# Row maxima taken bank by bank, four of each unit's pairs through a difference of keys: a four-layer attention kernel on one NeuronCore

## The chip, the cores and the metric

The kernel runs on one core of a Trainium2 chip. The time is device microseconds from the first to the last instruction of one execution. The engines named below are the tensor engine (PE, with its weight loads listed apart as PEld), VectorE (DVE), ScalarE (ACT), GpSimd (POOL) and SyncE (SP), which issues the DMAs. PSUM, where PE writes, has eight banks of 512 float32 values per partition.

## The reference

Four layers stand one behind the other on an input of 2048 tokens by 576 features: A, B, A, B. Each adds the output of an attention block over the layer-normed input. A has 32 heads of 18 features with keys and values of their own; in B all heads share one key and one value. There is no mask.

```python
def _A_ref(x, wqkv, wo):                      # D, H = 576, 32; Dh = 18
    qkv = (x @ wqkv).reshape(B, S, 3, H, Dh)  # q, k, v per head
    scores = einsum("bhqd,bhkd->bhqk", q, k) * Dh ** -0.5
    o = einsum("bhqk,bhkd->bhqd", softmax(scores), v)
    return o.reshape(B, S, D) @ wo
# _B_ref: the same with one k and one v for all heads
x = x + _A_ref(layernorm(x), ...); x = x + _B_ref(layernorm(x), ...)   # twice
```

So each layer computes 32 score matrices of 2048 by 2048, their row maxima, their exponentials, the row sums and the product with the values, in float32.

## The kernel before, in words

Each layer has three parts. First the layer norm, the transposes of x and the projections; q and k go to DRAM split into a coarse and a fine half, so that 18 features become 54 rows (coarse, fine, coarse for q; coarse, coarse, fine for k) and one product of 54 rows gives the score to float32 accuracy. Then the attention loop. Last the output projection of the layer, which runs into the norm of the next.

The attention loop goes over 16 pairs of heads; the first head's rows lie on partitions 0 to 63 and the second's on 64 to 127, so that the matmuls of the two heads use different halves of the tensor engine. A **unit** is one pair of heads and 512 queries; a layer has 64 units, and each takes four steps over the engines:

1. **Maxima.** For each head, four blocks of 128 queries by four blocks of 512 keys: 32 matmuls (L542), each of which fills one PSUM bank with scores, queries on the partitions. Two of them, side by side in a tile of two banks (`psm`, two such tiles rotate), are reduced by one VectorE instruction over 128 x 1024 values (L551) into two columns of `mx`.
2. **The maximum as rows.** VectorE takes the negative maximum of each four columns (L682), GpSimd splits it into halves, VectorE transposes it, and two sets of DMAs bring it through DRAM into two rows of the q operand, beside rows of ones in k. The contraction of the next step then gives score minus maximum.
3. **Exponentials.** 32 matmuls (L706), each 128 keys by 512 queries, into single banks (`pse`, three rotate), and 32 ScalarE exponentials (L710) into SBUF tiles `pt`.
4. **Values.** For each 512 queries, eight steps of four matmuls of 19 columns (18 features and a column of ones for the sum) on the four column groups of the tensor engine, summed into the bank `oacc` (L731). One ScalarE copy (L737) takes the sum out, and GpSimd and DMAs finish it.

PSUM thus holds four banks for maxima, three for exponentials and `oacc`. The tiles of the first and last part of a layer come from the same two rings.

The order on the tensor engine is written out by hand. `UNIT` is a list of phases; each names a run of **rows** (`m0` is the next maximum matmul of the first head, `e1` the next exponential matmul of the second) and a number of columns of step 4 that follow them. The list of before has twelve phases with 32 maxima, 32 exponentials and 4096 columns in all, that is one unit. The maxima run 14 steps (56 matmuls) ahead of the exponentials; these 56 are woven into the projections ahead of the loop, and at its end the 56 exponentials that are left run three to a phase with 384 columns. Small work (DMAs, sums, loads of the next weights) hangs in a table `todo` by step. Semaphores are put in by the framework, from what each instruction reads and writes; the engines work through their queues in order.

```python
UNIT = [("m0 m1 e0 e0 e1 m0 m1", 384), ("e0 m1 m0 e1 e0", 352), ...]   # twelve phases
        rows, cols = UNIT[phase % len(UNIT)]
        for kind, a in rows: exp_next(a) if kind == "e" else max_mm()
        if phase >= 2: pv_cols(cols)
```

## Time and profile before

| | |
|---|---|
| median of three runs | 5763.13 us (5759.74 to 5768.0) |
| the profiled execution: time, span | 5768.38 us, 5766.5 us |
| mean granted clock of the tensor engine | 0.996 |
| busy: PE, DVE, ACT, POOL | 99%, 89%, 79%, 30% of the span |
| L551, maxima on VectorE | 4096 instructions, 4736.5 us busy, 1219 ns each |
| L710, exponentials on ScalarE | 8192 instructions, 4288.9 us busy, 602 ns each |
| L542 and L706, score matmuls | 8192 each, 452 and 433 ns each |

Busy time is the time in which an engine has at least one instruction in flight; instructions of an engine that follow each other closely overlap in part, so busy time divided by their count can be less than the duration of one. The ends of matmuls are modelled, and float32 matmuls (step 4) appear as two instructions each. The chain is followed back from the last instruction, at each step to what released it.

### The profile page before, as it was taken

The numbers are of one execution on the slowest core, as the hardware profiler recorded it, in microseconds if no ns is written. First come the engines' busy times: TensorE is split into PE (matmuls) and PEld (weight loads), VectorE is DVE, ScalarE is ACT, GpSimd is POOL, SyncE is SP. The second block draws the span as 40 slices with busy tenths as digits, with TensorE's granted clock in tenths as the row PEclk, the third lists the DMA queues.
The fourth block names the chain that finished last, engine by engine and source line by source line (L and its number), as shares of the span: only waits on it lengthen the run. The fifth ranks groups of instructions, "written<-read, shape, count | busy, mean of one in ns | idle before, by whom it ended". The sixth has DMA issues, their size and how long they took to land.

```text
span 5766.5 us, 141306 instructions
## 1 busy us (share of the span) xinstructions
PE 5734.9 (99%) x57918; PEld 2923.1 (51%) x57918; DVE 5117.8 (89%) x5321; ACT 4581.1 (79%) x8872; POOL 1735.3 (30%) x2224
## 2 busy tenths in 40 slices
PE   9999999999999999999999999999999999999999
PEld 8644444444844444444685444444448444444446
DVE  4799999998699999999638999999977999999995
ACT  2588888888388888888625888888882888888885
POOL 3133232324233323233311423232332332323232
PEclk9999999999999999999999999999999999999999
DMA  6311111111420000001243111111114100010002
GB/s 201 106 46 32 35 32 36 32 33 23 126 66 24 22 23 20 23 20 24 59 169 91 40 35 33 34 33 34 31 33 129 52 23 23 23 23 20 23 14 77
DMA packets 250340, 276.96 MB, mean 48 GB/s; under 512 B 131732, under 2 KB 171924, under 8 KB 239972
## 3 DMA queue, kind: packets, MB, share of 16 engines
q1 hardware_dynamic: 249692, 267.92, 16.9%
q8 instruction: 455, 7.45, 0.6%
q14 instruction: 193, 1.58, 0.1%
HBM read 151.24 MB, written 112.56 MB: 46 GB/s over the span
## 4 chain that ended last, share of the span: by engine, by line
PE 96%; ACT 1%; DVE 1%; POOL 1%; DMA 1%; issue 0%; SPq 0%; POOLq 0%; ACTq 0%; DVEq 0%
PE oacc L731 36%; PE pse L706 24%; PE psm L542 23%; PE psn L224 6%; PE psq L394 6%; ACT pt L710 1%; DVE mx L551 1%; PE ps L216 0%; DMA raw<-in_B_wk_dram 0%; POOL big L170 0%; SPq L157 0%; PE oacc L217 0%; POOL os L745 0%; POOL os L767 0%; POOL os L144 0%
## 5 line engine op out<-in xcount | busy, mean ns | idle before, releaser
L551 DVE TENSOR_REDUCE mx<-psm 128x2 f32<-128x1024 f32 x4096 | 4736.5, 1219 | 173.5 <-PE psm L542 158.3
L710 ACT ACTIVATE pt<-pse 128x512 f32<-128x512 f32 x8192 | 4288.9, 602 | 538.3 <-PE pse L706 404.4
L542 PE MATMUL psm<-big 62*128 62x512 f32 x8192 | 2538.4, 452 | 6.9 <-DVE mx L551 6.8
L706 PE MATMUL pse<-big 64*128 64x512 f32 x8192 | 2494.8, 433 | 4.0 <-DMA big<-m_d 2.9
L731 PE MATMUL oacc<-pt,vbuf 128*19 128x320 f32 (+5 forms) x27664 | 1787.6, 361 | 5.2 <-ACT oc L737 5.2
L706 PEld LDWEIGHTS pse<-big 64*128 64x128 f32 x8192 | 1225.7, 185 | 861.4 <-ACT pt L710 675.7
L542 PEld LDWEIGHTS psm<-big 62*128 62x128 f32 x8192 | 1052.7, 184 | 815.2 <-DVE mx L551 645.0
L731 PEld LDWEIGHTS oacc<-pt,vbuf 128*19 128x19 f32 x27664 | 537.2, 98 | 784.1 <-issue 603.4
L144 POOL TENSOR_SCALAR hl<-neg 128x8 fp32r<-128x8 f32 x256 | 50.9, 199 | 2631.2 <-DVE neg L682 2631.2
L754 POOL TENSOR_TENSOR rl<-lt,mone 128x8 f32<-128x8 f32 x256 | 423.7, 1655 | 576.5 <-DMA lt<-os 576.5
L731 PE MATMUL oacc<-pt,vy 128*19 128x192 f32 (+2 forms) x9200 | 595.2, 361 | 0.0
L144 POOL TENSOR_SCALAR os<-oc 32x512 f32<-32x512 f32 x512 | 314.4, 614 | 138.2 <-ACT oc L737 96.2
L767 POOL TENSOR_TENSOR os<-os,rb 96x512 f32<-96x512 f32 x256 | 329.5, 1287 | 22.6 <-DMA rb<-r_d 21.8
L745 POOL TENSOR_TENSOR os<-os,oc 96x512 f32<-96x512 f32 x256 | 328.3, 1282 | 21.3
L731 PEld LDWEIGHTS oacc<-pt,vy 128*19 128x19 f32 x9200 | 195.7, 98 | 273.4 <-issue 213.4
L402 ACT ACTIVATE ev<-psq 128x512 fp32r<-128x512 f32 (+1 forms) x112 | 67.0, 598 | 324.7 <-PE psq L394 235.4
L224 PE MATMUL psn<-wsm,xx 128*128 128x288 f32 x2240 | 307.4, 296 | 0.0
L224 PEld LDWEIGHTS psn<-wsm,xx 128*128 128x128 f32 x2240 | 298.6, 188 | 10.4 <-issue 7.1
L408 DVE TENSOR_TENSOR ev<-psq,ev 128x512 fp32r<-128x512 f32 (+1 forms) x84 | 58.1, 691 | 215.6 <-ACT ev L402 202.5
L394 PE MATMUL psq<-yx,big 128*128 128x512 f32 (+2 forms) x826 | 197.5, 392 | 5.3 <-DVE ev L408 2.5
L394 PE MATMUL psq<-xx,big 128*128 128x512 f32 (+1 forms) x784 | 194.2, 397 | 0.0
L737 ACT ACTIVATE oc<-oacc 128x512 f32<-128x512 f32 x256 | 158.1, 618 | 30.4 <-PE oacc L731 30.4
(73 smaller groups left out, 1380.7 us busy)
## 6 DMA issues: line engine op xcount, KB each, us to landing
big<-qk_d SPq DMA_DIRECT2D x180, 432.0 KB
qk_d<-ev SPq DMA_DIRECT2D x96, 512.0 KB
qk_d<-ev SPq DMA_DIRECT2D x120, 256.0 KB
rb<-r_d SPq DMA_DIRECT2D x512, 36.0 KB
o_d<-os SPq DMA_DIRECT2D x512, 36.0 KB
m_d<-tr SPq DMA_DIRECT2D x1024, 2.0 KB
o<-o_d SPq DMA_DIRECT2D x64, 256.0 KB
big<-m_d SPq DMA_DIRECT2D x512, 4.0 KB
```

What stands on the lines that cost most here:

```text
L144: eng.tensor_scalar(dst, src, 1.0, 0.0, op0=OP.mult, op1=OP.add)
L224: nc.tensor.matmul(ps, lhs[:, xc, :], wsm[:, wc, h * 288:(h + 1) * 288], start=i == 0, stop=i == len(TERMS) - 1)
L394: nc.tensor.matmul(ps[:n].rearrange("p (u t) -> p u t", u=2)[:, us], w[:, wc, :n], xts[T][:, us, xc, :], start=(xc, wc) == TERMS[0], stop= ...
L542: nc.tensor.matmul(ps[:, slot], q[b:b + KM, c0:c0 + P], k[b:b + KM, kb * 512:(kb + 1) * 512], start=True, stop=True)
L551: nc.vector.reduce_max(mxs[p, u][:, r0:r1 + 1:r1 - r0], ps, axis=AX.X)
L706: nc.tensor.matmul(e, k[r:r + KE, kc * P:(kc + 1) * P], q[r:r + KE, u * 512:(u + 1) * 512], start=True, stop=True)
L710: nc.scalar.activation(pt, e, AF.Exp, scale=SCALE)
L731: nc.tensor.matmul(oacc[j:j + DH + 1, cs], v_of(kc)[:, 2 * p + a if is_a else 0, :], pts[p, u, i][:, cs], start=kc < 2 and c0 == 0, stop=k ...
L737: nc.scalar.activation(oc, oacc, AF.Copy)
L745: nc.gpsimd.tensor_tensor(t[:96], t[:96], oc[:96], op=OP.add)
L754: nc.gpsimd.tensor_tensor(rl, lts.pop((p, u)), mone, op=OP.pow)
L767: nc.gpsimd.tensor_tensor(t[:96], t[:96], rb[:96], op=OP.mult)
```

## The change

The score matmuls and everything else that used the two PSUM rings now use one tile of seven banks, `banks`, and helper functions hand out its banks by number: in the loop banks 0 to 3 for exponentials and 4 to 6 for maxima, in the tail of a layer all seven for exponentials, elsewhere 0 to 2 for single tiles and 3 to 6 for pairs.

In the loop each maximum matmul has a bank and a reader of its own. Of the 32 of a unit, 24 are reduced by VectorE one bank at a time. The other eight are four pairs a, b with the same queries and two blocks of keys. The row maximum of both is the maximum of a + relu(b - a); the matmul for b takes the difference of the two blocks of keys as its operand, ScalarE writes its relu to SBUF, and VectorE adds that to the matmul of a and takes the maximum in one instruction (which the build turns into two: the sum with its maximum, and a read of the accumulator). The first pair of heads of each layer has no differences and reduces all 32 bank by bank.

The differences of keys are made once per pair of heads (in B once per layer): DMAs bring the halves of the two blocks into `xx`, GpSimd subtracts and splits them, and DMAs take them through DRAM into rows of `xx`. The weight loads inside the loop now share one of the two `xh` buffers; the other holds the relu. `UNIT` has ten phases with the same 32 maxima, 32 exponentials and 4096 columns. The tail runs four exponentials and 512 columns per phase, and its last copies of `oacc` move to VectorE.

```diff
-UNIT = [("m0 m1 e0 e0 e1 m0 m1", 384), ("e0 m1 m0 e1 e0", 352), ...
+UNIT = [("m1 e0 e1 e0 m1 m0", 512), ("m0 e1 m1 e0 e1 m0", 480), ("e1 m0 m1 e0 e0 m0 e1", 416),
+        ("m1 m0 e1 e0 e1 m0", 224), ("e1 m0 m1 m1 e0", 544), ("m1 m0 e0 e1 e1 m0", 352), ("e0 m1 e1 m0 e0 m1", 416),
+        ("m0 e1 e1 m1 e0 m1 e0", 384), ("m1 m0 e1 e0 m0 e0 e1 m1 m0", 448), ("m0 e1 m1 e0 m1 e0", 320)]
+UNIT_X = (9, 16, 24, 31)
...
+    banks = psum.tile([P, 7, 512], F32, name="banks")
...
-    def mtile2(name):
-        return psum.tile([P, 2, 512], F32, tag="m", bufs=2, name=name)
-    def etile(name):
-        return psum.tile([P, 512], F32, tag="e", bufs=3, name=name)
+    at_bank = {"e": 0, "m": 0, "pair": 0}
+    layout = {"e": 3, "m": 4}
+    def mtile2():
+        at_bank["pair"] += 1
+        i = 3 + 2 * (at_bank["pair"] % 2)
+        return banks[:, i:i + 2]
+    def m1tile():
+        at_bank["m"] += 1
+        return banks[:, 4 + at_bank["m"] % 3]
+    def etile():
+        at_bank["e"] = (at_bank["e"] + 1) % layout["e"]
+        return banks[:, at_bank["e"]]
...
+            if diff:
+                nc.tensor.matmul(ps, q[b:b + 3 * DH, c0:c0 + P], kd(p)[b:b + 3 * DH], start=True, stop=True)
+            else:
+                nc.tensor.matmul(ps, q[b:b + KM, c0:c0 + P], k[b:b + KM, kb * 512:(kb + 1) * 512], start=True, stop=True)
...
+                if diff:
+                    t = relus[p, u, a, qc] = relu[:, :512]
+                    nc.scalar.activation(t, ps, AF.Relu)
+                elif (p, u, a, qc) in relus and kb == 0:
+                    t = relus.pop((p, u, a, qc))
+                    nc.vector.tensor_tensor_reduce(t, ps, t, 1.0, LOWEST, OP.add, OP.max, mx[:, r:r + 1])
+                else:
+                    nc.vector.reduce_max(mx[:, r:r + 1], ps, axis=AX.X)
...
+        def diff_split(p):
+            nc.gpsimd.tensor_tensor(d, hi1, hi0, op=OP.subtract)
+            nc.gpsimd.tensor_tensor(d, d, lo1, op=OP.add)
+            nc.gpsimd.tensor_tensor(d, d, lo0, op=OP.subtract)
+            copy(nc.gpsimd, hi, d)
+            nc.gpsimd.tensor_tensor(lo, d, hi.bitcast(F32), op=OP.subtract)
...
-                    max_mm()
+                    max_mm(True)
...
+        layout.update(e=7)
         while sum(e_next) < 4 * ns:
             run_todo(LEAD + sum(e_next) // 4)
-            for _ in range(min(3, 4 * ns - sum(e_next))):
+            for _ in range(min(4, 4 * ns - sum(e_next))):
                 exp_next(int(e_next[0] > e_next[1]))
-            pv_cols(384)
+            pv_cols(512)
```

## The prediction

> **What bounds the kernel now.** I read the page first, then the groups of one long stretch of the loop, the chain there, and single rows.

> ```profile
> span 5766.5 us, 141306 instructions
> ...
> PE 5734.9 (99%) x57918; PEld 2923.1 (51%) x57918; DVE 5117.8 (89%) x5321; ACT 4581.1 (79%) x8872; POOL 1735.3 (30%) x2224
> ...
> PE 96%; ACT 1%; DVE 1%; POOL 1%; DMA 1%; issue 0%; SPq 0%; POOLq 0%; ACTq 0%; DVEq 0%
> ...
> L551 DVE TENSOR_REDUCE mx<-psm 128x2 f32<-128x1024 f32 x4096 | 4736.5, 1219 | 173.5 <-PE psm L542 158.3
> L710 ACT ACTIVATE pt<-pse 128x512 f32<-128x512 f32 x8192 | 4288.9, 602 | 538.3 <-PE pse L706 404.4
> L542 PE MATMUL psm<-big 62*128 62x512 f32 x8192 | 2538.4, 452 | 6.9 <-DVE mx L551 6.8
> ```

> The last line says that a maximum matmul hardly ever waits for its bank: 6.9 us in all. The groups from 600 to 1368 us:

> ```profile
> L551 DVE TENSOR_REDUCE mx<-psm 128x2 f32<-128x1024 f32 x636 | 735.3, 1219 | 26.4 <-PE psm L542 24.3 <-PE pse L706 1.0
> ...
> L737 ACT ACTIVATE oc<-oacc 128x512 f32<-128x512 f32 x40 | 24.7, 617 | 0.6 <-PE oacc L731 0.6
> ```

> 40 copies of `oacc`, one a unit, in 768 us: a unit takes 19.2 us. VectorE is busy 18.4 of them (735.3/40). The chain in this stretch lies on the tensor engine alone; its pieces (start, length) show two phases:

> ```profile
> 803.23 0.23 PE psm L542
> 803.46 0.24 PE pse L706 x2
> 803.70 0.82 PE oacc L731 x8
> ...
> 808.01 0.43 PE pse L706 x2
> 808.44 0.24 PE psm L542 x2
> 808.68 0.22 PE pse L706
> 808.90 0.56 PE oacc L731 x8
> ```

> Rows of the two heads run side by side; the first pair of a phase costs 0.43 us, each further one 0.235. Then 416 columns of step 4 take 0.82 and 256 take 0.56, so c columns take 0.14 + 1.63c/1000. The twelve phases need 35 such pairs: 12 x 0.43 + 23 x 0.235 + 12 x 0.14 + 4096 x 0.00163 = 18.9 us of the 19.2. The tensor engine's order is the bound and stalls 0.3 us a unit; VectorE is close behind.

> **The change: the rows.** From the new list of phases alone one would expect a gain (a rival, below). But before a row can be priced, one must know what it waits for. Waits come from the framework, and the built program lists them:

> ```
> L811 Matmult banks<-big 128x512 [waits DVE_49]
> L598 Matmult banks<-big 128x512 [waits Activation_49]
> L811 Matmult banks<-big 128x512 [waits DVE_49]
> L598 Matmult banks<-big 128x512 [waits Activation_49]
> L836 Matmult oacc<-pt,vbuf 19x416 x4
> L598 Matmult banks<-big 128x512 [waits DVE_49]
> L811 Matmult banks<-big 128x512 [waits DVE_49]
> L811 Matmult banks<-big 128x512 [waits Activation_49]
> ```

> L811 is an exponential row (banks 0 to 3, which only ScalarE reads there), L598 a maximum row. An exponential row behind a maximum row waits for VectorE, which reads none of its banks; a maximum row behind an exponential row waits for ScalarE. By the values of the semaphores it is the reader of the row directly ahead, in all but some 170 of the 16384 rows. So the seven banks are guarded as one tile: a row may start only when the row before it has been read. In the program of before each ring slot is a tile of its own, and `pse` waits for ScalarE alone. One place there has the same form, the two halves of a `psq` pair in the first layer, of which the second waits for the subtraction that reads the first:

> ```profile
> 20.98 0.69 DVE L408 TENSOR_TENSOR ev<-psq,ev 128x512 fp32r<-128x512 f32 x1 [1.75 <-ACT ev L402]
> ...
> 21.73 0.19 PEld L394 LDWEIGHTS psq<-yx,big 128*128 128x128 f32 x1
> ```

> That load starts 0.06 after the subtraction's end (21.67), and its record carries a wait for VectorE's semaphore, where the loads around it carry none. So such a wait for a neighbouring bank does reach the chip, though here it cost almost nothing.

> The price of a row is now a round trip, and rows of before that waited show its parts:

> ```profile
> 799.52 0.60 ACT L710 ACTIVATE pt<-pse 128x512 f32<-128x512 f32 x1
> ...
> 800.18 0.18 PEld L706 LDWEIGHTS pse<-big 64*128 64x128 f32 x1 [0.25 <-ACT pt L710]
> ...
> 769.54 0.51 PE L706 MATMUL pse<-big 64*128 64x512 f32 x2
> ...
> 770.08 2.58 ACT L710 ACTIVATE pt<-pse 128x512 f32<-128x512 f32 x5 [0.18 <-PE pse L706]
> ```

> From the end of a reader to the next weight load 0.06; from there to the start of the next reader 0.54. With the 0.60 of ScalarE an exponential row costs 1.20 us, and a relu row the same. For VectorE over 512 values I take the 0.69 of the subtraction above (between 0.61, half of 1.219, and 0.69 nothing changes that matters): 1.29. The sum with its maximum is not in the trace. Below, the plain 0.69 bounds it; above, 0.69 and a second full pass; I take 0.69 plus the 0.18 of the smallest reduction, since its second instruction reads one value:

> ```profile
> L682 DVE TENSOR_REDUCE neg<-mx 128x8 f32<-128x32 f32 x40 | 7.0, 176 | 0.0
> ```

> That makes 1.47 (1.29 to 1.98, over 960 of them +0.5 or -0.2 ms). The loops hold 4 x (2048 - 56) = 7968 exponentials and as many maxima, of which 960 are relus, 960 sums and 6048 plain. Sum: 8928 x 1.20 + 6048 x 1.29 + 960 x 1.47 = 19.93 ms, where the same 249 units (7968/32) took 249 x 19.2 = 4.78 ms. Behind a waiting row PE holds the rest of the phase and its columns of step 4; ScalarE and VectorE, which wait for just those rows, idle meanwhile. Step 4 waits for nothing new and runs while the last row of a phase is read; only the widest phases stick out (512 columns: 0.33 + 0.97 = 1.30 against 1.29), 0.05 ms. At the full clock the loops thus gain 15.2 ms in length.

> **The clock.** A round trip leaves the tensor engine idle most of the time: 64 matmuls of 0.5 and ten phases of step 4 of about 0.75 are some 39 us of an 80 us unit, 49% busy. These rows (a stretch, PE busy, ..., granted clock) show what followed such stretches:

> ```profile
> 1323.30:1326.76 3.46, 1.72 (x24) 0.68 (x22) 1.73 (x3) 1.83 (x4) 3.04 (x7) 1.00 0.05 15
> 1326.76:1330.17 3.41, 3.41 (x25) 1.35 (x21) 2.08 (x3) 1.73 (x4) 1.22 (x2) 0.50 0.10 21
> 1436.00:1439.40 3.40, 2.11 (x26) 0.72 (x28) 0.00 (x0) 2.58 (x6) 0.94 (x2) 1.00 0.25 76
> 1439.40:1442.80 3.40, 3.40 (x27) 0.87 (x19) 2.86 (x2) 2.70 (x6) 2.97 (x3) 0.50 0.07 19
> 800.00:803.40 3.40, 3.40 (x40) 1.62 (x36) 3.37 (x5) 3.28 (x8) 0.52 (x3) 1.00 0.00 0
> ```

> After 50% and 62% busy the next 3.4 us are granted half; at 100% all. So I expect half the clock through most of the loop, and its price stands in the halved stretch:

> ```profile
> 1328.70 0.79 PE L706 MATMUL pse<-big 64*128 64x512 f32 x2
> ...
> 1329.53 1.58 ACT L710 ACTIVATE pt<-pse 128x512 f32<-128x512 f32 x3 [0.68 <-PE pse L706]
> ```

> 0.83 from load to reader in place of 0.54. Rows then cost 1.49, 1.58 and 1.76: 8928 x 1.49 + 6048 x 1.58 + 960 x 1.76 = 24.55 ms. Step 4 doubles its stream (512 columns: 0.54 until it starts and 1.85 against a row of 1.58) and sticks out by about 5 us a unit, 1.3 ms. Loops: 25.85 - 4.78 = +21.1 ms. At half clock a unit is 66% busy by the same count, no more than what lost the clock at 1436, so I expect it to stay lost.

> [...]

> **The rest.** The layers' tails hold 224 exponentials; before, ScalarE was their bound at some 0.52 each (4288.9/8192), so +0.15 ms at the full clock, +0.27 at half. Outside the loops the tiles of the two rings share `banks` too:

> ```profile
> L402 ACT ACTIVATE ev<-psq 128x512 fp32r<-128x512 f32 (+1 forms) x112 | 67.0, 598 | 324.7 <-PE psq L394 235.4
> ...
> L745 POOL TENSOR_TENSOR os<-os,oc 96x512 f32<-96x512 f32 x256 | 328.3, 1282 | 21.3
> ```

> The 112 projection tiles of the first line, 64 transposes, 64 tiles of the output projection, some 40 of the values and 112 pairs of maxima; each now holds up the next matmul until it is read: 392 x about 1.5 us (a read of 0.6 to 1.3 and two handovers, at places where two tiles in turn hid it) = +0.6 ms. The differences (nine DMAs and five GpSimd operations a pair of heads), the single weight buffer on SP, and the relu buffer are hidden in a unit of 80 us, in which POOL's 6 and SP's share do not grow; uncovered, five operations of at most the 1.28 us above would be 6 us for each of 32 pairs, 0.2 ms. The copy on ScalarE and the small VectorE work fall into gaps.

> Sum at half clock: 5.77 + 21.1 + 0.27 + 0.6 = 27.7 ms; at full clock 5.77 + 15.2 + 0.15 + 0.6 = 21.7 ms. The profiled execution (5768.38) is 5 us above the median, which is nothing here.

> **Rivals.** (1) Serial rows at the full clock throughout: 21.7 ms. For it: the row 800 to 803 and every long stretch of before keep it; against it: both half-busy stretches. (2) The clock comes and goes by windows, half the time each: about 24.7 ms, the mean. (3) The other side, faster: the rows do not wait for each other on the chip, each only for its own bank. Then the new list decides: 34 pairs in ten phases, 10 x 0.43 + 24 x 0.235 + 10 x 0.14 + 4096 x 0.00163 = 18.0 us, 0.9 below before. The other two engines then follow closely:

> ```profile
> 768.81 1.08 ACT L710 ACTIVATE pt<-pse 128x512 f32<-128x512 f32 x2
> ...
> 802.54 2.35 DVE L551 TENSOR_REDUCE mx<-psm 128x2 f32<-128x1024 f32 x2
> ```

> Two exponentials start 1.08 - 0.60 = 0.48 apart, two reductions 2.35 - 1.22 = 1.13. ScalarE needs 37 x 0.48 = 17.8; VectorE, at 0.60 for half the elements, 24 x 0.60 + 4 x 0.9 + 0.3 = 18.3, so the unit would take 18.3 to 18.6: 240 units x 0.6 to 0.9 less, 5.55 to 5.62 ms. What decides is the price of one wait: a unit has 0.9 us in hand, so a single row in 64 that makes its round trip uncovered takes all of it. Against it stands the list of waits.

> [...]

> **Chances.** Half clock 0.59; (2) 0.14; (1) 0.18; (3) and the like 0.07, of which 0.01 ends within 0.2%, about what three runs of this kernel tell from no change; other slower ways 0.02. Predicted: 27.7 ms, with its own range of 26 to 29. Faster holds 0.06, slower the serial cases' 0.93. The range that leaves out less than 2 in 10 reaches from (1), less 0.5 for the prices, to the half-clock sum with the dearer sum: 21.2 to 28.9 ms.

> **What would show it.** In the profile after: PE busy well below 70%; ScalarE and VectorE below 35%; the wait of the maximum rows for ScalarE and of exponential rows for VectorE as the largest; one exponential, then one reduction, never two in flight; a unit of about 80 us at clock 1.0 or 100 us at 0.5; the granted clock near 0.5. The prediction is wrong if exponential rows wait only for ScalarE and the unit is near 18 us.

## The result and the profile after

The changed kernel takes 27969.8 us (median of 4 runs, 27967.2 to 27972.7) where the kernel before takes 5763.5 us on the same chip: a ratio of 4.855, with a 95% interval of 4.849 to 4.861. The forecast was 27,700 us.

The page of the changed kernel (busy time and share of the span, the granted clock in 40 slices, and the four largest groups with their idle time):

```profile
span 27969.5 us, 139507 instructions
...
PE 17529.7 (63%) x53790; PEld 6364.6 (23%) x53790; DVE 5393.8 (19%) x9313; ACT 5816.6 (21%) x9824; POOL 1823.7 (7%) x2386
...
PEclk6555555555655555555565555555556555555555
...
L811 PE MATMUL banks<-big 64*128 64x512 f32 x8192 | 6482.0, 791 | 5489.1 <-DVE mx L610 2574.4
L815 ACT ACTIVATE pt<-banks 128x512 f32<-128x512 f32 x8192 | 4890.7, 597 | 18289.5 <-PE banks L811 18242.1
L598 PE MATMUL banks<-big 62*128 62x512 f32 x7232 | 5622.3, 788 | 4187.8 <-ACT pt L815 2774.0
L610 DVE TENSOR_REDUCE mx<-banks 128x1 f32<-128x512 f32 x6048 | 4180.9, 691 | 19348.0 <-PE banks L598 19348.0
```

ScalarE and VectorE are busy only 1.2 and 0.3 ms longer than before (5817 against 4581 us, 5394 against 5118). Ahead of their main groups they now idle for 18.3 and 19.3 ms, waiting for the matmul: the new time is idle time on both readers. On the tensor engine the busy time has tripled, for two reasons. At half its clock a matmul of 512 columns takes 791 ns where it took 433 to 452. And the rows of the two heads no longer run side by side: before, 8192 maximum rows of 452 ns filled only 2538.4 us, and now 7232 of 788 ns fill 5622.3. What the rows wait for stands in the view of the waits (total, times, longest):

```profile
PEld banks L811 <- DVE mx L610: 5015.0, 4028, 1.6
PEld banks L598 <- ACT pt L815: 4815.9, 4008, 1.5
PEld banks L811 <- ACT pt L815: 3499.4, 2916, 1.5
```

The first two lines are the waits that nothing in the algorithm asks for. An exponential row (L811) uses banks that VectorE never reads in the loop, yet half of all exponential rows wait for VectorE; maximum rows wait for the exponentials of ScalarE as often. One stretch of the timeline shows how it looks (start, length, instruction, and in brackets the idle time before it and what ended it):

```profile
15002.04 0.79 PE L811 MATMUL banks<-big 64*128 64x512 f32 x1 [0.69 <-ACT pt L815]
15002.87 0.60 ACT L815 ACTIVATE pt<-banks 128x512 f32<-128x512 f32 x1 [0.88 <-PE banks L811]
15003.52 0.28 PEld L811 LDWEIGHTS banks<-big 64*128 64x128 f32 x1 [1.20 <-ACT pt L815]
15003.52 0.79 PE L811 MATMUL banks<-big 64*128 64x512 f32 x1 [0.69 <-ACT pt L815]
15004.35 0.60 ACT L815 ACTIVATE pt<-banks 128x512 f32<-128x512 f32 x1 [0.88 <-PE banks L811]
15005.00 0.28 PEld L598 LDWEIGHTS banks<-big 62*128 62x128 f32 x1 [1.19 <-ACT pt L815]
15005.00 0.79 PE L598 MATMUL banks<-big 62*128 62x512 f32 x1 [0.69 <-ACT pt L815]
15005.83 0.69 DVE L610 TENSOR_REDUCE mx<-banks 128x1 f32<-128x512 f32 x1 [5.32 <-PE banks L598]
15006.57 0.28 PEld L598 LDWEIGHTS banks<-big 62*128 62x128 f32 x1 [1.29 <-DVE mx L610]
```

There is never more than one row in flight: matmul, reader, next matmul. An exponential row takes 15005.00 - 15003.52 = 1.48 us, a maximum row 15006.57 - 15005.00 = 1.57. Two copies of the accumulator, one a unit, start 104.4 us apart:

```profile
14601.79 0.60 ACT L843 ACTIVATE oc<-oacc 128x512 f32<-128x512 f32 x1 [2.65 <-PE oacc L836]
14706.18 0.60 ACT L843 ACTIVATE oc<-oacc 128x512 f32<-128x512 f32 x1 [2.65 <-PE oacc L836]
```

### The profile page after: what moved, and what is told of

It is laid out like the page before. It is cut to its first block, busy times and chain, and to the rows that moved or that the text cites. A ratio compares the mean times of both kernels' runs of the same rounds, so it can differ in the third digit from the quotient of the medians.

```text
span 27969.5 us, 139507 instructions
## 1 busy us (share of the span) xinstructions
PE 17529.7 (63%) x53790; PEld 6364.6 (23%) x53790; DVE 5393.8 (19%) x9313; ACT 5816.6 (21%) x9824; POOL 1823.7 (7%) x2386
## 5 line engine op out<-in xcount | busy, mean ns | idle before, releaser
L811 PE MATMUL banks<-big 64*128 64x512 f32 x8192 | 6482.0, 791 | 5489.1 <-DVE mx L610 2574.4
L815 ACT ACTIVATE pt<-banks 128x512 f32<-128x512 f32 x8192 | 4890.7, 597 | 18289.5 <-PE banks L811 18242.1
L598 PE MATMUL banks<-big 62*128 62x512 f32 x7232 | 5622.3, 788 | 4187.8 <-ACT pt L815 2774.0
L610 DVE TENSOR_REDUCE mx<-banks 128x1 f32<-128x512 f32 x6048 | 4180.9, 691 | 19348.0 <-PE banks L598 19348.0
L811 PEld LDWEIGHTS banks<-big 64*128 64x128 f32 x8192 | 2329.3, 284 | 10088.4 <-DVE mx L610 5015.0
L598 PEld LDWEIGHTS banks<-big 62*128 62x128 f32 x7232 | 2024.0, 284 | 7861.5 <-ACT pt L815 4815.9
L836 PE MATMUL oacc<-pt,vbuf 128*19 128x416 f32 (+1 forms) x24560 | 3040.0, 626 | 3.5 <-DVE oc L172 3.5
L836 PE MATMUL oacc<-pt,vy 128*19 128x288 f32 (+3 forms) x8176 | 1006.6, 626 | 0.0
L608 DVE CUSTOM_DVE_ANT_0 relu<-banks,relu 128x512 f32<-128x512 f32 x960 | 664.0, 692 | 1748.7 <-PE banks L598 1748.7
L836 PEld LDWEIGHTS oacc<-pt,vbuf 128*19 128x19 f32 x24560 | 674.7, 128 | 1401.3 <-issue 1396.3
L596 PE MATMUL banks<-xx,big 54*128 54x512 f32 x960 | 759.9, 792 | 352.9 <-DVE mx L610 188.1
L836 PEld LDWEIGHTS oacc<-pt,vy 128*19 128x19 f32 x8176 | 259.6, 135 | 500.7 <-issue 500.7
L875 POOL TENSOR_TENSOR os<-os,rb 96x512 f32<-96x512 f32 x256 | 324.5, 1268 | 20.5 <-DMA rb<-r_d 19.4
L853 POOL TENSOR_TENSOR os<-os,oc 96x512 f32<-96x512 f32 x256 | 321.8, 1257 | 21.3
```

Source lines behind the costliest of these rows:

```text
L596: nc.tensor.matmul(ps, q[b:b + 3 * DH, c0:c0 + P], kd(p)[b:b + 3 * DH], start=True, stop=True)
L598: nc.tensor.matmul(ps, q[b:b + KM, c0:c0 + P], k[b:b + KM, kb * 512:(kb + 1) * 512], start=True, stop=True)
L608: nc.vector.tensor_tensor_reduce(t, ps, t, 1.0, LOWEST, OP.add, OP.max, mx[:, r:r + 1])
L610: nc.vector.reduce_max(mx[:, r:r + 1], ps, axis=AX.X)
L811: nc.tensor.matmul(e, k[r:r + KE, kc * P:(kc + 1) * P], q[r:r + KE, u * 512:(u + 1) * 512], start=True, stop=True)
L815: nc.scalar.activation(pt, e, AF.Exp, scale=SCALE)
```

## The experiments

Two theories stood at the start. By mine, the seven banks that are cut from one tile are guarded as one, which makes the rows serial, and the half-idle tensor engine then loses half its clock. By the rival, the change's own work costs the time: its single reads, its differences or its list of ten phases. A third question came out of the answer: what is the change worth when its rows are not serial?

**The change with seven tiles.** Each bank becomes a tile of its own; where one instruction used two banks, two instructions stand.

```
-    banks = psum.tile([P, 7, 512], F32, name="banks")
+    banks = [psum.tile([P, 512], F32, name=f"bank{i}") for i in range(7)]
...
-        return banks[:, at_bank["e"]]
+        return banks[at_bank["e"]]
...
-        nc.vector.tensor_tensor(xc, ps[:, :, :288], xc, op=OP.add)
+        for h in range(2):
+            nc.vector.tensor_tensor(xc[:, h], ps[h][:, :288], xc[:, h], op=OP.add)
```

> The changed kernel, its seven banks now seven tiles of one bank each; where it used two banks by one instruction, two instructions of one bank stand. Theory (the guard over one tile makes the rows serial): exponential rows wait for ScalarE alone and only for their own bank, a unit takes 18.3 to 18.6 us instead of 104.4, the granted clock is back near 1.0, and the time is 5.55 to 5.65 ms. Rival (the work of the change itself, its differences, its 32 single reads a unit or its ten phases, is what takes the time): the time stays above 20 ms. Between them (the guard is the cause, but the ten phases or the two readers are worth less than their sum): 5.7 to 6.2 ms.

Measured: 5844.4 us, 1.0152 times the kernel before (1.0138 to 1.0166). The page of this kernel:

```profile
PE 5802.0 (99%) x53790; PEld 2959.3 (51%) x53790; DVE 4938.2 (85%) x9489; ACT 4939.9 (85%) x9840; POOL 1827.7 (31%) x2386
...
PEclk9999999999999999999999999999999999999999
```

And from its timeline two copies of the accumulator, one unit apart:

```profile
810.60 0.62 ACT L847 ACTIVATE oc<-oacc 128x512 f32<-128x512 f32 x1
...
830.13 0.62 ACT L847 ACTIVATE oc<-oacc 128x512 f32<-128x512 f32 x1
```

What the exponential rows wait for (total, times, longest) is now ScalarE; on VectorE's reductions of the loop they wait twice, 1.7 us in all:

```profile
PEld bank L815 <- ACT pt L819: 351.4, 526, 1.2
```

One declaration, with the instructions that it splits, takes back 22.1 of the 22.2 ms. All of the change's work is still in this kernel, so the rival falls; the clock is back as well, at 0.997. The time is the one of the case between, 5.7 to 6.2 ms: the unit takes 19.5 us and not the 18.3 to 18.6 that I had put on it, and even without the guard the change loses 1.5%. Why, is taken up below.

**The kernel before with one tile.** Nothing but the ring slots is changed:

```
+    banks = psum.tile([P, 7, 512], F32, name="banks")
...
-        return psum.tile([P, 2, 512], F32, tag="m", bufs=2, name=name)
+        at_bank["m"] += 1
+        i = 3 + at_bank["m"] % 2 * 2
+        return banks[:, i:i + 2]
...
-        return psum.tile([P, 512], F32, tag="e", bufs=3, name=name)
+        at_bank["e"] += 1
+        return banks[:, at_bank["e"] % 3]
```

> The kernel before, its order, its pairs of maxima and its ring sizes unchanged; only its seven banks are cut from one tile as in the changed kernel, where they were ring slots of their own. Theory (the guard over the tile alone makes the rows serial): 32 exponentials at 1.49 us and 16 pairs at 0.47 + 0.83 + 1.22 + 0.06 = 2.58 us make 89 us a unit at half clock, 23.0 to 25.5 ms in all; at the full clock 1.20 and 2.06 make 71 us and 19.5 ms. Rival (the guard is harmless and the changed kernel's own list or its single reads make it slow): 5.7 to 5.9 ms.

Measured: 23329 us (4.05 times), a granted clock of 0.529 and 85.4 to 86.1 us a unit. Its timeline has the same picture as that of the changed kernel, here with the exponential row at 3003.65 held until the pair's reduction is over:

```profile
3002.38 1.22 DVE L556 TENSOR_REDUCE mx<-banks 128x2 f32<-128x1024 f32 x1 [2.37 <-PE banks L547]
...
3003.65 0.28 PEld L711 LDWEIGHTS banks<-big 64*128 64x128 f32 x1 [1.82 <-DVE mx L556]
```

With the run before, this shows the cause from both sides: the one tile makes a kernel slow that has none of the change's work, and the change's work is not slow without it.

**Four banks in one tile.** Seven tiles, but the four banks of the exponentials are cut from one again:

```
+    quad = psum.tile([P, 4, 512], F32, name="quad")
+    banks = [quad[:, i] for i in range(4)] + [psum.tile([P, 512], F32, name=f"bank{i}") for i in range(3)]
```

> The changed kernel with seven tiles, except that the four banks of the exponentials are cut from one tile again; the three of the maxima stay apart. Theory (the guard serialises exactly the rows within one tile): the exponentials alone go one at a time, 32 x 1.20 = 38.4 us a unit and 10.6 to 11.2 ms at the full clock, 32 x 1.49 = 47.7 us and 12.8 to 13.4 ms at half; exponential rows wait for ScalarE only, maxima for VectorE and the relus' ScalarE. Rival (one shared tile of any kind makes all rows serial): near 28 ms. Rival (only a tile with two reading engines is guarded too widely): 5.55 to 5.8 ms.

Measured: 15354 us, clock 0.554, some 56 us a unit. Both rivals fall: only the rows of the shared tile are serial, and one reading engine is enough for it, since in the loop their loads wait for ScalarE:

```profile
PEld quad L816 <- ACT pt L820: 6778.5, 6127, 2.0
```

The size was off: 12.8 to 13.4 ms was expected at half clock. I had priced 32 exponential rows one after the other (47.7 us) and forgotten what stands between them. From one exponential row to the next it takes 1.48 us (median of 1093, from 600 to 3400 us) where nothing of step 4 lies between, but 2.46 us (median of 497) where step 4 does, ten times a unit; 32 x 1.48 + 10 x 0.98 = 57 us. In these gaps step 4 and the maximum rows beside it run one after the other and together last longer than the wait for the reader, under which the sum had hidden them: 2.03 us with one maximum row ahead of step 4, 2.83 with two behind it.

**The clock: work that adds nothing.** The changed kernel, its one tile untouched, with matmuls of zeros behind every row but a phase's last, one, two or three (FILL):

```
             for n, (kind, a) in enumerate(rows):
+                if n and pv_at[0] % 4096:
+                    for j in range(FILL):
+                        nc.tensor.matmul(oacc[:DH + 1, j * P:j * P + P], zeros[:, :DH + 1], zeros,
+                                         start=False, stop=False)
```

Three of them:

> The changed kernel with its one tile of seven banks; behind every row but a phase's last, while a unit's sum is open in the accumulator, stand three matmuls of zeros (19 x 128 outputs each, they add nothing to it), which need no wait of a row. In the trace of the changed kernel a matmul of zeros by zeros with 128 columns takes about 0.4 us at half clock (two passes of 0.2), so 0.2 at the full clock: three of them fill most of the 0.66 to 0.75 us in which the tensor engine waits for a reader. Theory (the half clock is granted because the tensor engine idles a third of the time): the clock comes back to about 1.0, rows take 1.20, 1.29 and 1.47 us, and the time falls to 21.5 to 23 ms although work was added. Rival (the half clock has another cause and stays): a row then holds 0.79 + 3 x 0.4 = 2.0 us of tensor work instead of 1.49 to 1.58, and the time grows to about 34 ms.

One:

> The changed kernel with one matmul of zeros behind every row in place of three. At half clock the row and its filler are 0.79 + 0.4 = 1.2 of 1.49 to 1.58 us, 78% busy; at the full clock 0.7 of 1.20 to 1.29, 56%. Theory (a share of busy time this low does not bring the clock back): the clock stays near 0.52 and the time near 28 ms. Rival (78% is enough to be granted the full clock from time to time): a clock of 0.6 to 0.8 and 23 to 27 ms.

Two:

> Two matmuls of zeros behind every row. At half clock 0.79 + 0.8 = 1.6 us fill a row of 1.49 to 1.58 entirely, so the full clock should be granted; at the full clock 0.9 of 1.20 to 1.29 are busy, 72%, and whether it is kept is open. Kept: clock above 0.9, 21.5 to 23 ms. Lost and granted in turn: clock 0.6 to 0.8, 24 to 27 ms. Never granted: 28 to 30 ms.

Measured: 23119 us with three (clock 0.892), 26950 with two (0.653, a single time), 27952 with one (0.519, a single time). Adding 71,000 matmul passes made the kernel 4.85 ms faster. One and two came out as expected (for two, the case of a clock lost and granted in turn); three ended just above the expected 23 ms, with a clock of 0.89 and not 1.0. The busy time of the engines and the granted clock, from the page of the kernel with three:

```profile
PE 21168.3 (92%) x125214; PEld 11052.0 (48%) x125214; DVE 5398.9 (23%) x9313; ACT 5791.4 (25%) x9824; POOL 1825.3 (8%) x2386
...
PEclk8899898988799999889889999998988988898988
```

From the page of the one with two:

```profile
PE 24322.4 (90%) x101406; PEld 10459.9 (39%) x101406; DVE 5398.8 (20%) x9313; ACT 5800.1 (22%) x9824; POOL 1825.0 (7%) x2386
...
PEclk6656656566766666666687566756657666665666
```

And of the one with one:

```profile
PE 23966.1 (86%) x77598; PEld 8012.5 (29%) x77598; DVE 5397.6 (19%) x9313; ACT 5817.2 (21%) x9824; POOL 1823.9 (7%) x2386
...
PEclk6555555555655555555565555555556555555555
```

On one chip and with the same data the clock went from 0.519 with one filler to 0.892 with three. So the half clock came from the idle time between the rows and not from the chip or from the kernel's data. The rows of the kernel with three, from its timeline, now run at the full clock:

```profile
3000.41 0.50 PE L599 MATMUL banks<-big 62*128 62x512 f32 x1
...
3001.69 0.49 PE L812 MATMUL banks<-big 64*128 64x512 f32 x1
...
3002.88 0.49 PE L599 MATMUL banks<-big 62*128 62x512 f32 x1
```

1.28 us for a maximum row and 1.19 for an exponential one: the 1.29 and 1.20 of the prediction's full-clock sum. The total stays 1.4 ms above the 21.7 ms of that sum. Nearly all of it lies in the loop: its units take 85.2 us (median) where the sum has 19.93 ms / 249 = 80.0, which over 249 units is 1.3 ms. The clock is still a tenth short: from 700 to 6000 us 85% of the rows have the full-clock length and the others that of half clock. How the 1.3 ms divides between the clock and the fillers themselves was not measured.

**What the change is worth with seven tiles.** Two parts taken back one at a time. Without differences (all 32 maxima reduced on VectorE):

```
-UNIT_X = (9, 16, 24, 31)
+UNIT_X = ()
...
-                for d, f in ((0, diff_in), (3, diff_split), (5, diff_out), (8, diff_rows)):
-                    at(b + d, f, p + 1)
```

> Seven tiles as in the run beside it, but without differences: all 32 maxima of a unit are plain reductions of one bank on VectorE, and the DMAs and GpSimd operations that form the differences are gone. Theory (a reduction of one bank starts about 0.60 us after the one before it, and VectorE is the bound): 32 x 0.60 + 0.3 = 19.5 us a unit, 5.80 to 5.95 ms, VectorE above 95% busy. Rival (the tensor engine's list of phases bounds the unit and the differences are not needed for it): 18.3 to 18.6 us, 5.55 to 5.65 ms, as with differences.

And with the list of twelve phases of the kernel before, copied over the ten:

```
-UNIT = [("m1 e0 e1 e0 m1 m0", 512), ("m0 e1 m1 e0 e1 m0", 480), ...
+UNIT = [("m0 m1 e0 e0 e1 m0 m1", 384), ("e0 m1 m0 e1 e0", 352), ...
```

> Seven tiles and differences as in the first run of this set, with the list of twelve phases of the kernel before in place of the ten. Theory (the tensor engine's order is the bound, and 12 x 0.43 + 23 x 0.235 + 12 x 0.14 + 4096 x 0.00163 = 18.9 us is its price): 19.0 to 19.4 us a unit, 5.70 to 5.82 ms, the tensor engine above 97% busy. Rival (the list of phases does not matter, the relief of VectorE does): as with ten phases, 5.55 to 5.65 ms.

Measured: 6076.6 us (1.0554, 1.0540 to 1.0569) and 6234.3 us (1.0829, 1.0815 to 1.0844), units of 20.5 and 21.2 us. Both were slower than either theory allowed, so something was in none of them. Measuring each phase of a unit from its first row to its step 4, against the price 0.43 + 0.235 for each further pair, shows it. With seven tiles and the change's list, seven of the ten phases are within 0.1 us of their price, and three are not: 1.42 for 0.90, 1.24 for 0.90 and 1.74 for 1.37. With the twelve phases, the three that hold four maxima take 1.71, 1.71 and 1.83 for 1.14, and a short one 0.96 for 0.67. Without differences four phases of the ten break: 1.32, 1.51 and 1.28 for 0.90, and 2.31 for 1.37. The timeline of the seven tiles in the first of these phases shows what breaks it:

```profile
805.66 0.68 DVE L609 CUSTOM_DVE_ANT_0 relu<-bank,relu 128x512 f32<-128x512 f32 x1
...
806.45 0.60 ACT L606 ACTIVATE relu<-bank 128x512 f32<-128x512 f32 x1 [0.27 <-DVE mx L609]
...
807.10 0.18 PEld L599 LDWEIGHTS bank<-big 62*128 62x128 f32 x1 [0.47 <-ACT relu L606]
```

A relu waits for the one relu buffer, which the sum before it is still reading; the relu therefore reads its bank late; and the third maximum row waits for that bank, alone, when its pair has long gone by. The relu buffer is not the only cause, since the same phase and three others break without any relu, when VectorE reads all maxima. With three banks for maxima, one late reader is enough to break a pair.

**The split turned round.** The change's own list and differences, four banks for maxima and three for scores:

```
-        return banks[4 + at_bank["m"] % 3]
+        return banks[3 + at_bank["m"] % 4]
...
-        layout.update(e=4)
```

> The seven tiles with the changed kernel's own list of ten phases and its differences; only the split of the banks is turned round, four for maxima and three for scores. Theory (a list fits one split; the ten phases issue up to three scores before the first maximum, and a fourth score now waits for the first one's reader): unit about 22 us, 6.4 to 6.5 ms. Rival (the maxima's banks are the scarce ones whatever the list): faster than with three for maxima, below 5.84 ms.

Measured: 6519.3 us (1.1325, 1.1310 to 1.1341), just above the expected 6.5 ms, and 22.4 us a unit. This list fits the one split and not the other; that another list can run well with four and three is shown next.

**A list that fits.** From the prices measured so far I looked for an order in which no row finds its bank unread, with four banks for maxima, three for scores and three differences a unit. The best one:

```
+UNIT = [("e1 m0 m0 m1 e0 e1", 384), ("e0 e1 m1 m0 m0 e1", 512), ("m1 e0 e0 m1 m1 e0", 256), ("m1 e0 e0 m1", 320),
+        ("m0 e1 e0 m1 m0 e1", 320), ("e1 m0 e0 m1", 96), ("m0 e1 e0 m1", 384), ("e1 m0 e1 m0 m1 e0", 416),
+        ("e0 m1 m1 e0 e0 m1", 256), ("e1 m0 e1 m0", 288), ("m0 e1 m0 e1 m0 e1", 480), ("e0 m1 m1 m0 e0 e1", 384)]
+UNIT_X = (10, 17, 25)
```

> Seven tiles, differences, and a new list of twelve phases made from the prices seen in the runs so far (a pair 0.43 and 0.235 us, 477 ns from one ScalarE read to the next, 598 ns from one VectorE reduction to the next, 0.54 from a row to its reader, 0.06 back): four banks for maxima and three for scores, three differences a unit instead of four, maxima and exponentials spread so that no row should find its bank unread. Theory (with seven tiles the three phases with broken pairs are what the changed kernel's list loses): 32 pairs in 12 phases, 12 x 0.43 + 20 x 0.235 + 12 x 0.14 + 4096 x 0.00163 = 18.2 us, so 18.2 to 18.6 us a unit and 5.50 to 5.62 ms, faster than the kernel before. Rival (three banks for scores or the shared readers break pairs again): 19.2 us or more and at least 5.76 ms.

And a second list that came out nearly as well, of eleven phases:

> As the list beside it, with eleven phases (32 pairs: 11 x 0.43 + 21 x 0.235 + 11 x 0.14 + 4096 x 0.00163 = 17.9 us) and one phase of step 4 of 96 columns. Theory (broken pairs decide, and the longer phases break a few): 18.2 to 18.6 us a unit, 5.50 to 5.62 ms. Rival: 19.2 us or more and at least 5.76 ms.

Measured: 5605.3 us, 0.9735 times the kernel before (0.9722 to 0.9749), and 5630.2 us, 0.9781 (0.9768 to 0.9795). The first is 2.6% faster than the kernel before; the second ended just above its expected 5.62 ms. Its unit is 18.6 us (median) like the first one's, but one of its phases takes 1.18 for 0.90, and single units of 19.8 us are among them. In the first, every phase is within 0.1 us of its price. All three engines stand close to the limit (768 us of its loop):

```profile
sum 768.00, PE 766.40 PEld 350.05 DVE 740.48 ACT 748.33 POOL 281.36; mean PE 766.40 PEld 350.05 DVE 740.48 ACT 748.33 POOL 281.36
```

The same list without differences says what these are worth:

> The faster list of twelve phases with four banks for maxima and three for scores, without differences: all 32 maxima are plain reductions on VectorE, and the DMAs and GpSimd operations that form the differences are gone. Theory (with this list VectorE, at 598 ns from one reduction to the next, becomes the bound): 32 x 0.598 + 0.28 = 19.4 us a unit, 5.80 to 5.90 ms, slower than the kernel before. Rival (the differences bring nothing, the new list and the seven tiles are the whole gain): 18.5 us and about 5.60 ms.

Measured: 5777.2 us, 1.0031 (1.0018 to 1.0044), units of 19.2 to 19.4 us. The unit is the expected one; the time lies just under the expected 5.80 ms, within 0.5% of the kernel before. VectorE's reductions, 1% of the chain with the differences, now make up 42% of it:

```profile
PE 53%; DVE 43%; POOL 1%; issue 1%; DMA 1%; ACT 0%; SPq 0%; DVEq 0%; POOLq 0%; ACTq 0%
DVE mx L620 42%; PE oacc L849 18%; PE bank L608 12%; PE bank L824 11%; PE bank L264 6%; PE bank L435 6%; POOL big L210 0%; PE bank L256 0%; DMA raw<-in_A_wqkv_dram 0%; DMA raw<-in_B_wq_dram 0%; DVE mx L629 0%; DVE tr L809 0%; DVE neg L800 0
```

So with banks that are guarded one by one, and with this list, the differences bring 172 us (5777.2 - 5605.3), and without them the kernel is not faster than before. The list was made for a unit with differences; whether another one does better without them was not tried.

## Why the prediction was right, and where it was off

- **The serial rows.** Right, and shown from both sides by the first two experiments. The two crossed waits were to be the largest of the rows' waits, and they are (5015.0 and 4815.9 us of weight loads).
- **The prices of the rows.** At half clock 1.49 and 1.58 were given; 1.48 and 1.57 were measured. The sum with its maximum was given 1.76, and its row takes 1.58: 14626.78 - 14625.20 in the rows below. The accumulator's read overlaps the sum: it is over at 14626.72, only 0.01 after the main instruction (14626.71), and the next weight load starts 0.06 later, as behind a plain reduction. The prediction had put it behind the sum with its whole length. 960 of these at 0.18 too much are 0.17 ms.

```profile
14625.20 0.79 PE L598 MATMUL banks<-big 62*128 62x512 f32 x1 [0.78 <-DVE mx L610]
14626.02 0.69 DVE L608 CUSTOM_DVE_ANT_0 relu<-banks,relu 128x512 f32<-128x512 f32 x1 [0.88 <-PE banks L598]
14626.64 0.08 DVE L608 DVE_READ_ACCUMULATOR2_ANT mx<- 128x1 f32 x1
14626.78 0.28 PEld L598 LDWEIGHTS banks<-big 62*128 62x128 f32 x1 [1.30 <-DVE mx L608]
```

- **Step 4.** Given some 5 us a unit beyond the rows; measured 104.4 - (36 x 1.48 + 24 x 1.57 + 4 x 1.58) = 7.1 us. This term was too small by about 0.5 ms over 249 units. All rows together had been priced 0.3 ms too dear (half of it the sum rows), which hid more than half of it; that the total came within 1% owes something to this.
- **The clock.** Right: 0.518 over the span, 0.50 in the loop with the tensor engine 62% busy (from 700 to 6800 us). The step that a unit 66% busy would not win the clock back holds with much room: the kernel with one filler is 86% busy and stays at 0.52. Two details of the reasoning were weaker than they looked. 66% is not "no more than" the 62% of the row at 1436; with the prediction's own unit of 25.85 ms / 249 = 104 us the count gives 63%. And its two rows were not the rule: of the 16 stretches of 3.41 us of the kernel before that were 40 to 80% busy at the full clock, 9 were followed by half clock. Half clock held in the changed kernel without a long gap: from 700 to 6800 us no row waits longer than 1.6 us, and all of that stretch is at half clock.
- **The rest.** 0.27 ms for the tails and 0.6 ms for tiles outside the loops were given. Span less 249 units is 27969.5 - 25995.6 = 1974 us after and 5766.5 - 4780.8 = 986 us before: +0.99 ms for the 0.87. The trace also tells the two apart. From the last maximum row of a layer to its last exponential row, the four tails take 401.8 us where they took 127.7, which is the 0.27 ms given. From the last exponential row of a layer to the first of the next, with both ends of the span, it is 1590.8 us for 851.3: +0.74 ms where 0.6 was given.
- **The rivals.** The full clock throughout (21.7 ms) and the mixed clock (24.7 ms) did not come about in the changed kernel. Even with three fillers, 92% busy, the clock came to 0.892 and not to 1.0.
- **The range.** Its upper end, 28.9 ms, does not follow from the sum that it names: 27.7 plus the 0.5 of the dearer sum is 28.2. The measured time lies inside either.
- **The faster rival's size was wrong.** It gave 18.3 to 18.6 us a unit and 5.55 to 5.62 ms for rows that wait for their own bank only; the chip gave 19.5 us and 5.84 ms. The step that failed is the phases' price for the new list, 18.0 us, which lets every row find its bank free. The terms beside it held (477 ns from one ScalarE read to the next against 0.48, 598 ns for a reduction against 0.60). The prediction did name the point that decides, 0.9 us in hand against one uncovered row, but did not look whether three banks keep to it: three phases lost 0.52, 0.34 and 0.37 us. Had the rows not been serial, the change would still have been slower, by 1.5%, and the chance of a gain should have been smaller than given.

## What to carry to other kernels

Look at what the guard of a buffer covers before counting what runs beside what: banks cut from one tile may all wait for each other, and the waits in the built program say so before any run. An order written by hand for one number of buffers need not fit another; compare each phase with its price, and a broken pair stands out at once. Where an engine's waits are short but many, look at the granted clock as well: here waits of at most 1.6 us went with a clock of 0.518, and bringing most of it back (0.892) took 4.85 ms off a loss of 22.2.

## What the runs showed of the hardware

I had not expected the clock to be so hard to win back. Three stretches of the loop follow (stretch, its length, busy time of PE, PEld, DVE, ACT and POOL with the number of instructions, granted clock, share of the DMA engines, GB/s). With one filler the tensor engine is 87% busy and is granted 0.51:

```profile
3000.00:3200.00 200.00, 173.52 (x556) 54.52 (x559) 37.55 (x65) 42.99 (x72) 14.75 (x19) 0.51 0.03 9
```

With two it is 91% busy and is granted 0.68:

```profile
9000.00:9200.00 200.00, 182.68 (x783) 76.51 (x782) 40.06 (x71) 44.70 (x76) 11.50 (x14) 0.68 0.03 7
```

With three it is 95% busy and is granted 0.97:

```profile
3000.00:3100.00 100.00, 94.56 (x605) 49.30 (x603) 24.45 (x41) 26.52 (x45) 5.75 (x7) 0.97 0.01 2
```

These shares are at whatever clock was granted, and a row looks busier at half clock: the matmul of an exponential row takes 0.79 of its 1.48 us there, and 0.49 of 1.19 at the full clock. The mean share is not the right measure either: over 600 to 6900 us the kernels with two and with three fillers are both 92% busy, and are granted 0.64 and 0.89.

| stretch of 3.41 us | under 40% busy | 40 to 80% | 80% and more |
|---|---|---|---|
| at full clock: followed by half clock | 272 of 272 | 435 of 1144 | 0 of 8573 |
| at half clock: followed by full clock | 0 of 30 | 0 of 9602 | 704 of 13110 |

So all 8573 stretches of 80% and more at the full clock kept it here, but such a share was not enough to bring it back: with three fillers 317 of 791 such stretches at half clock led back, with one only 83 of 6860. What tells those stretches apart, these runs do not settle.
